# Strassen's scheme for the first FFN product of the last two groups of 512 tokens, in an fp32 attention and FFN kernel

## The chip, the cores and the metric

The kernel runs on one core of a Trainium2 chip. Its engines work side by side (in the profiled run of the kernel before TensorE is busy 96% of the span, VectorE 61% and GpSimd 46%) and are written short in the profiles: TensorE is PE (matmuls) and PEld (its loading of weights), VectorE is DVE, ScalarE is ACT, GpSimd is POOL. SBUF is the memory that holds their operands, and PSUM the one that holds the sums of the matmuls. The metric is device time in microseconds (us) of one execution. A time quoted here is the median of a kernel's runs.

## The reference

```python
batch, n_heads, seq, head_dim = 8, 8, 576, 64         # q, k, v in fp32
n_tokens, d_model, d_ff = 4608, 512, 2048

scores = q @ k.T / 8
scores = where(scores >= max(scores) - tau, scores, -1e9)
attn = exp(scores - max(scores)); attn /= sum(attn) + 1e-9
x = (attn @ v), heads joined: 4608 x 512
h = x @ w_in                                          # 4608 x 2048, the first product
g = where(h > 0, h, exp(min(h, 0)) - 1)               # ELU
out = g @ w_out                                       # the second product
```

## The kernel before

TensorE works in fp32. The kernel cuts the 4608 tokens into nine **groups** of 512, and each group into two **blocks** of 256. Attention of one batch element and the FFN of earlier groups are interleaved by hand. When attention ends, two groups are left, which are computed with nothing else to do: this is the **tail** of the kernel, and the change acts in it alone.

The PSUM pools: the score tile is one tile of four slices of 512 columns, `f` has three separate tiles of 512 columns, `t` has one.

```python
    banks.close()
    for name, bufs in (("s", 1), ("f", 3), ("t", 1)):
        psum[name] = ctx.enter_context(tc.tile_pool(name=f"ps_{name}2", bufs=bufs, space=PSUM))
```

The first product of a block, plainly: for a **unit** `u` (slices `u` and `u + 8` of the 16 slices of the hidden layer) 8 matmuls of 128x128 by 256 columns, then the ELU in three steps on three engines.

```python
    def ffn1(c, u):                       # c: block, u: unit
        def part(k):
            ft = u + k * NU
            ...
            for j in range(KJ):
                nc.tensor.matmul(loc["ph"][:, k], w_in_sb[:, j, ft * P : (ft + 1) * P],
                                 xts[g][:, j, hf * CT : (hf + 1) * CT], start=(j == 0), stop=(j == KJ - 1))
        def exp():
            ...
            nc.scalar.activation(loc["g"], loc["h"], AF.Exp)
        def minus():
            nc.gpsimd.tensor_scalar(loc["g"], loc["g"], 1.0, -1.0, ALU.mult, ALU.add)
        def elu():
            nc.vector.scalar_tensor_tensor(loc["g"], loc["g"], 0.0, loc["h"], ALU.min, ALU.max)
            if u % 2 and c >= PLAIN:
                sums(c, u - 1)            # sums of g for the second product, on GpSimd
```

The second product uses Strassen's scheme (in Winograd's form) already: seven products in place of eight, collected in three accumulators X, Y, Z. The same order serves the change.

```python
    ORDER = ((("g", 0, 0), ("w", 0, 0), "X", True), (("g", 1, 1), ("t", 2), "Z", True), (("g", 1, 0), ("w", 1, 0), "X", False),
             (("s", 1), ("t", 0), "Y", True), (("s", 0), ("w", 0, 1), "Z", True), (("s", 2), ("t", 1), "Y", False),
             (("s", 3), ("w", 1, 1), "Z", False))
```

The end of the program:

```python
        finish_units(after, slice(0, None))
        xts[B] = xpool.tile([P, KJ, MAIN], FP32, name="xt")
        nc.sync.dma_start(xts[B], xtail.rearrange("j p n -> p j n"))
        push_ffn(B)
        while pending or units:
            finish_units(ffn_halves(1), slice(0, None))
            run_extra(99)
```

## Time and profile before

| | before |
|---|---|
| time, first three of the six runs | 1452.35 us (1450.76 to 1452.42) |
| mean granted clock of TensorE, profiled run | 0.995 |
| tail: first matmul of the last two groups to the last one | 207.2 us |
| first product of one group (512 tokens) | 55.3 us |
| second product of one group | 48.35 us |

"Granted clock" is the share of TensorE's full clock that the hardware grants; it is recorded over the whole run. In the kernel before the record falls to 0.50 in three stretches, of 3.41, 6.83 and 3.41 us, between 149.0 and 193.4 us, and is 1.00 from there to the end of the work. A row of a timeline is: start in us, length in us, engine, source line, operation, output tile and input tiles, shapes, how many records are joined in the row, and in brackets the idle time ahead of it with what ended it. A row of the chain of waits is: start, length, engine, output tile, line. The prediction below shows the lines of this profile that the argument rests on.

### The profile page before, as it was taken

Reading aid. Unit: us, or ns where it says so; the run is one execution under the profiler, and the core shown is the slowest. Engines: PE = TensorE matmul, PEld = TensorE weight load, DVE = VectorE, ACT = ScalarE, POOL = GpSimd, SP = SyncE. Lnnn points to the kernel's source line nnn. Section 1 sums busy time; section 2 is a strip of 40 time slices with the busy share of each in tenths; the row PEclk is TensorE's granted clock in tenths of the full one; section 3 lists DMA queues with packets and bytes.
Section 4 is the critical chain, followed back from the end, with each engine's and each line's share of the span. In section 5 each row is a group of like instructions: output and inputs, shape, how many; then the busy total and the mean of one; then the engine's idle time right before and its main releaser. Section 6 shows DMA issues by size and latency. Waiting matters only on the chain.

```text
span 1449.4 us, 20329 instructions
## 1 busy us (share of the span) xinstructions
PE 1391.5 (96%) x6822; PEld 1037.2 (72%) x6822; DVE 878.9 (61%) x1910; ACT 439.7 (30%) x780; POOL 667.7 (46%) x1194
## 2 busy tenths in 40 slices
PE   7988778999999999999999999999999999999998
PEld 4555534647777777777777777777777778888887
DVE  6887665567676766677676767676767674111111
ACT  5665554323222322223222323232323231100100
POOL 4665554546444454535363626363535443313422
PEclk9999899999999999999999999999999999999999
DMA  4344442177677676667676767666767765100000
GB/s 95 78 93 117 111 123 84 51 193 188 184 185 195 174 202 183 190 181 185 183 197 171 189 190 191 182 189 180 195 182 192 192 172 148 45 15 8 8 15 15
DMA packets 298903, 205.44 MB, mean 142 GB/s; under 512 B 206384, under 2 KB 270384, under 8 KB 298800
## 3 DMA queue, kind: packets, MB, share of 16 engines
q1 hardware_dynamic: 298800, 204.15, 52.9%
q8 instruction: 54, 0.88, 0.2%
q14 instruction: 49, 0.40, 0.1%
HBM read 119.87 MB, written 84.21 MB: 141 GB/s over the span
## 4 chain that ended last, share of the span: by engine, by line
PE 82%; DVE 8%; POOL 4%; ACT 3%; issue 2%; DMA 1%; SPq 0%; POOLq 0%; DVEq 0%; ACTq 0%
PE ph L393 33%; PE po L494 24%; PE sc L220 12%; PE pv L347 8%; DVE w L247 2%; PE pv L343 2%; PE po L459 2%; ACT e L235 2%; POOL wtop L141 2%; DVE mx L230 2%; PE rt L259 1%; POOL w L256 1%; DVE wtop L136 1%; POOL nb L231 1%; DVE w_out_sb L145 1%
## 5 line engine op out<-in xcount | busy, mean ns | idle before, releaser
L393 PE MATMUL ph<-xt,w_in_sb 128*128 128x256 f32 x2304 | 521.5, 383 | 3.5 <-DVE w_in_sb L145 3.5
L393 PEld LDWEIGHTS ph<-xt,w_in_sb 128*128 128x128 f32 x2304 | 433.3, 190 | 83.9 <-issue 21.0
L235 ACT ACTIVATE e<-sc,nb,keep 128x576 f32<-128x576 f32 x288 | 227.6, 829 | 439.2 <-POOL nb L231 438.0
L230 DVE TENSOR_REDUCE mx<-sc 128x2 f32<-128x1152 f32 (+1 forms) x176 | 199.9, 1136 | 229.1 <-PE sc L220 229.0
L256 POOL TENSOR_SCALAR w<-w,rs 128x576 f32<-128x576 f32 x288 | 219.1, 771 | 223.5 <-DVE rs L250 217.3
L247 DVE SCALAR_TENSOR_TENSOR w<-sc,th,e 128x576 f32<-128x576 f32 x288 | 226.8, 815 | 78.3 <-ACT e L235 53.8
L220 PE MATMUL sc<-kT,qT 64*128 64x288 f32 x1024 | 180.3, 437 | 18.9 <-DVE w L247 9.1
L404 POOL TENSOR_SCALAR g<-g 128x512 f32<-128x512 f32 x144 | 89.7, 623 | 200.5 <-ACT g L401 199.3
L307 DVE STREAM_TRANSPOSE x<-w 128x512 f32<-128x512 f32 (+1 forms) x350 | 181.2, 567 | 0.9 <-POOL w L256 0.9
L231 POOL TENSOR_SCALAR nb<-mx,nkeep 128x2 f32<-128x2 f32 (+1 forms) x176 | 51.7, 294 | 265.1 <-DVE mx L230 257.6
L401 ACT ACTIVATE g<-ph 128x512 f32<-128x512 f32 x144 | 86.0, 597 | 266.2 <-PE ph L393 266.2
L408 DVE SCALAR_TENSOR_TENSOR g<-g,ph 128x512 f32<-128x512 f32 x144 | 97.0, 674 | 112.7 <-POOL g L404 112.6
L220 PEld LDWEIGHTS sc<-kT,qT 64*128 64x128 f32 x1024 | 99.3, 189 | 86.0 <-issue 53.1
L494 PE MATMUL po<-t,s 128*128 128x256 f32 x512 | 122.8, 386 | 4.5 <-DVE u L514 4.5
L494 PE MATMUL po<-w_out_sb,s 128*128 128x256 f32 x512 | 120.1, 384 | 0.0
L494 PE MATMUL po<-w_out_sb,g 128*128 128x256 f32 x512 | 117.7, 379 | 0.0
L494 PEld LDWEIGHTS po<-t,s 128*128 128x128 f32 x512 | 94.5, 190 | 28.9 <-DVE u L514 8.9
L494 PEld LDWEIGHTS po<-w_out_sb,s 128*128 128x128 f32 x512 | 95.4, 190 | 19.7 <-issue 4.7
L494 PEld LDWEIGHTS po<-w_out_sb,g 128*128 128x128 f32 x512 | 97.3, 190 | 13.9
L424 POOL TENSOR_TENSOR s<-g 128x256 f32<-128x256 f32 x128 | 93.2, 728 | 12.9 <-DVE g L408 12.9
L347 PE MATMUL pv<-wTb,vm 128*64 128x320 f32 x512 | 76.7, 439 | 0.0
L350 ACT COPY xt<-pv 128x256 f32<-128x256 f32 x64 | 23.8, 372 | 159.3 <-PE pv L347 159.2
(64 smaller groups left out, 1129.0 us busy)
## 6 DMA issues: line engine op xcount, KB each, us to landing
there<-x SPq DMA_DIRECT2D x500, 144.0 KB, 3.5
wTb<-there SPq DMA_DIRECT2D x75, 576.0 KB, 4.4
wTa<-there SPq DMA_DIRECT2D x50, 576.0 KB, 3.7
qm<-in_q_dram SPq DMA_DIRECT2D x128, 72.0 KB, 2.6
km<-in_k_dram SPq DMA_DIRECT2D x128, 72.0 KB, 3.6
vm<-in_v_dram SPq DMA_DIRECT2D x64, 128.0 KB, 2.5
wst<-in_moe_w_in_dram SPq DMA_DIRECT2D x16, 512.0 KB, 4.2
wst<-in_moe_w_out_dram SPq DMA_DIRECT2D x16, 512.0 KB, 3.8
```

The source lines that it names most:

```text
L220: nc.tensor.matmul(scs[h][:, a, :HALF], qs[r], kT[r, k0 : k0 + HALF], start=True, stop=True)
L230: nc.vector.tensor_reduce(st["mx"][:, cs], src[:, :, :, :HALF], axis=AX.XY, op=ALU.max)
L235: nc.scalar.activation(e, st[h][:, :, :HALF], AF.Exp, bias=st["nb"][:, h : h + 1], scale=keep)
L247: nc.vector.scalar_tensor_tensor(wv, sc[:, :, :HALF], st["th"][:, h : h + 1], e, ALU.is_ge, ALU.mult, accum_out=sm[:, h : h + 1])
L256: nc.gpsimd.tensor_scalar(wv, wv, st["rs"][:, h : h + 1], 1.0, ALU.mult, ALU.mult)
L307: nc.vector.transpose(x[:, :, c0 : c0 + nc_], src.rearrange("p (c g n) -> p g c n", c=nc_, n=T))
L347: nc.tensor.matmul(pv[h * D : (h + 1) * D, g0 * T : g1 * T], vm[:, h, c], wT[:, g0:g1, h * (NC + 1) + c], start=False, stop=(c == NC - 1), ...
L393: nc.tensor.matmul(loc["ph"][:, k], w_in_sb[:, j, ft * P : (ft + 1) * P], xts[g][:, j, hf * CT : (hf + 1) * CT], start=(j == 0), stop=(j = ...
L404: nc.gpsimd.tensor_scalar(loc["g"], loc["g"], 1.0, -1.0, ALU.mult, ALU.add)
L408: nc.vector.scalar_tensor_tensor(loc["g"], loc["g"], 0.0, loc["h"], ALU.min, ALU.max)
L424: nc.gpsimd.tensor_tensor(out, x, y, op)
L494: nc.tensor.matmul(cur[c, place], lhs, rhs, start=(begins and u == 0), stop=(u == NU - 1), skip_group_check=True)
```

## The change

The first product of the last two groups goes by the seven products as well, for 512 tokens at a time. That needs, per unit, three new sums of weights and one in place (`first_sums`), four sums of the input per group (`input_sums`), and per unit six sums and two copies of the results in PSUM ahead of the ELU. The tiles that attention leaves free (`qm`, `km`, `qT`, `kT`, `e`, `w`, `vm`, `wTa`, `wTb`) hold the sums. Bookkeeping and the second product's small changes are cut.

```diff
@@ at the end of the program
+        def first_sums(u):
+            f0, f1 = (slice(f * P, (f + 1) * P) for f in (u, NU + u))
+            a11, a12, a21 = w_in_sb[:, :2, f0], w_in_sb[:, 2:, f0], w_in_sb[:, :2, f1]
+            s1, s2, s4 = sums_in[u] = [rooms.pop(0).rearrange("p (k f) -> p k f", k=2) for _ in range(3)]
+            nc.vector.tensor_tensor(s1, a21, w_in_sb[:, 2:, f1], ALU.add)
+            nc.vector.tensor_tensor(s2, s1, a11, ALU.subtract)
+            nc.vector.tensor_tensor(a21, a11, a21, ALU.subtract)
+            nc.vector.tensor_tensor(s4, a12, s2, ALU.subtract)
+
+        for u in range(5):
+            first_sums(u)
         while pending or units:
             finish_units(ffn_halves(1), slice(0, None))
             run_extra(99)
 ...
+        def input_sums(g):
+            (b11, b12), (b21, b22) = ...
+            nc.vector.tensor_tensor(t3, b22, b12, ALU.subtract)
+            nc.vector.tensor_tensor(t2, t3, b11, ALU.add)
+            nc.vector.tensor_tensor(t4, b21, t2, ALU.subtract)
+            nc.vector.tensor_tensor(b12, b12, b11, ALU.subtract)
+
+        def first_product(g, u):
 ...
+            if u % 2:
+                sc = psum["s"].tile([P, 2, 2, 512], FP32, name="sc").rearrange("p a b n -> p (a b) n")
+                X, Y, Z = (sc[:, i, :CT] for i in range(3))
+            else:
+                X, Y, Z = (psum["f"].tile([P, 512], FP32, name="po", tag="f")[:, :CT] for i in range(3))
 ...
+            product(a11, b11, X, True)
+            p1 = kept("s1", X)                        # copy on ScalarE
+            product(a22, t4, Z, True)
+            w1 = kept("w1", Z, p1)                    # sum on VectorE, as u2 and t5
+            product(a12, b21, X, False)
+            nc.scalar.copy(h[:, 0, 0], X)
+            product(s2, t2, Y, True)
+            u2 = kept("u2", Y, p1)
+            product(s1, t1, Z, True)
+            t5 = kept("t5", Z, p1)
+            product(s3, t3, Y, False)
+            nc.vector.tensor_tensor(h[:, 0, 1], Y, w1, ALU.add)
+            nc.vector.tensor_tensor(h[:, 1, 1], Y, t5, ALU.add)
+            product(s4, b22, Z, False)
+            nc.vector.tensor_tensor(h[:, 1, 0], Z, u2, ALU.add)
+            for c in range(2):
+                ...
+                nc.scalar.activation(gt, hc, AF.Exp)
+                nc.gpsimd.tensor_scalar(gt, gt, 1.0, -1.0, ALU.mult, ALU.add)
+                nc.vector.scalar_tensor_tensor(gt, gt, 0.0, hc, ALU.min, ALU.max)
+            if u % 2:
+                sums(2 * g, u - 1)
+                run_extra(99)
+
+        input_sums(B - 1)
 ...
+        for g in (B - 1, B):
+            ...
+            for u in range(NU):
+                if g < B and u + 2 in range(5, NU):
+                    first_sums(u + 2)
+                first_product(g, u)
+            ... second products of both blocks; input_sums(B) after the first group's first block
```

More of the change, by code (lines that the diff above doesn't have):

```diff
@@ L397, in exp @@
             if u == 0:
-                gs[c] = gpool.tile([P, NU, 2, 2, P], FP32, name="g")
-            loc["g"] = gs[c][:, u].rearrange("p j i t -> p (j i t)")
+                gs[c] = [gpool.tile([P, NU, 2, 2, P], FP32, name="g")]
+            loc["g"] = hidden(c, u, 1).rearrange("p u j i t -> p (u j i t)")
             loc["h"] = loc["ph"].rearrange("p k t -> p (k t)")
@@ L412, in ffn1, with hidden, sums @@
         return [lambda: part(0), lambda: part(1)], (exp, minus, elu)
-    def sums(c, u):
-        g = gs[c]
+    def hidden(c, u, n):
+        for g in gs[c]:
+            if u < g.shape[1]:
+                return g[:, u : u + n]
+            u -= g.shape[1]
+    def sums(c, u, engines=(nc.gpsimd,) * 4):
+        g = hidden(c, u, 2)
         def one(k):
@@ L419, in one @@
                 ss[c] = late["x"].tile([P, 4, NU, P], FP32, name="s", bufs=1)
-            (a11, a21), (a12, a22) = ([g[:, u : u + 2, j, i] for i in range(2)] for j in range(2))
+            (a11, a21), (a12, a22) = ([g[:, :, j, i] for i in range(2)] for j in range(2))
             s1, s2, s3, s4 = (ss[c][:, i, u : u + 2] for i in range(4))
@@ L423, in one @@
                              (s3, a11, a21, ALU.subtract), (s4, a12, s2, ALU.subtract))[k]
-            nc.gpsimd.tensor_tensor(out, x, y, op)
+            engines[k].tensor_tensor(out, x, y, op)
         extra.extend((0.8, c, lambda k=k: one(k)) for k in range(4))
@@ L458, in run @@
             for ft in range(4 * part + 2 * k, 4 * part + 2 * k + 2):
-                nc.tensor.matmul(cur[c, i][:, :DM], gs[c][:, ft % NU, ft // NU, i], w_out_sb[:, ft],
+                nc.tensor.matmul(cur[c, i][:, :DM], hidden(c, ft % NU, 1)[:, 0, ft // NU, i], w_out_sb[:, ft],
                                  start=(ft == 0), stop=(ft == NFT - 1))
@@ L488, in part @@
             for u in range(k * NU // 2, (k + 1) * NU // 2):
-                lhs = gs[c][:, u, left[1], left[2]] if left[0] == "g" else ss[c][:, left[1], u]
+                lhs = hidden(c, u, 1)[:, 0, left[1], left[2]] if left[0] == "g" else ss[c][:, left[1], u]
                 if right[0] == "w":
@@ L548, in behind @@
             values(pr, 0 if i == 1 else 1)
-        if i == NB - 1 and (pr + 1) % NPAIR == 0:
+        if i == NB - 1 and (pr + 1) % NPAIR == 0 and pr + 1 < NP:
             push_ffn(pr // NPAIR)
@@ L693, with pieces_of @@
         finish_units(after, slice(0, None))
-        xts[B] = xpool.tile([P, KJ, MAIN], FP32, name="xt")
-        nc.sync.dma_start(xts[B], xtail.rearrange("j p n -> p j n"))
-        push_ffn(B)
+        def pieces_of(pool, name, shape, n, times=1, bufs=None):
+            for _ in range(times):
+                t = pool.tile(shape, FP32, name=name, bufs=bufs)
+                if len(shape) > 2:
+                    axes = " ".join("abc"[: len(shape) - 1])
+                    t = t.rearrange(f"p {axes} -> p ({axes})")
+                for x in range(0, t.shape[1] - n + 1, n):
+                    yield t[:, x : x + n]
+        QN = 2 * P
+        rooms = [*pieces_of(raw, "qm", [P, S // T, T], QN), *pieces_of(raw, "km", [P, S // T, T], QN),
+                 *pieces_of(qkp, "qT", [P, S], QN, 2), *pieces_of(qkp, "kT", [P, TAIL + S], QN, 2),
+                 *pieces_of(att, "e", [P, 2, HALF], QN, 2), *pieces_of(wpool[0], "w", [P, 2 * S], QN)]
+        sums_in = {}
+        def first_sums(u):
[8 more added lines that the diff above has]
+            first_sums(u)
         while pending or units:
@@ L699 @@
             run_extra(99)
+        wide, narrow = wtp.tile([P, 3 * NT, NCH, T], FP32, name="wTb"), wtp.tile([P, 2 * NT, NCH, T], FP32, name="wTa")
+        wide, narrow = (t.rearrange("p g c n -> p (g c n)") for t in (wide, narrow))
+        g2 = [t.rearrange("p (u j i t) -> p u j i t", j=2, i=2, t=P) for t in (wide[:, : 12 * QN], narrow[:, : 4 * QN])]
+        rooms += [wide[:, 12 * QN : 13 * QN], narrow[:, 8 * QN : 9 * QN], *pieces_of(raw, "vm", [P, 2, NC, D], QN, bufs=2)]
+        t2, t4 = (narrow[:, x * QN : (x + 2) * QN].rearrange("p (k t) -> p k t", k=2) for x in (4, 6))
@@ new lines @@
+        (t3,) = pieces_of(raw, "vm", [P, 2, NC, D], 2 * QN, bufs=2)
+        t3 = t3.rearrange("p (k t) -> p k t", k=2)
+        hs = [h.rearrange("p (c j t) -> p c j t", c=2, j=2) for h in pieces_of(late["x"], "x", [P, NT, NCH, T], 4 * QN, 2, 2)]
+        def input_sums(g):
+            (b11, b12), (b21, b22) = ([xts[g][:, k : k + 2, t : t + CT] for t in (0, CT)] for k in (0, 2))
+            nc.vector.tensor_tensor(t3, b22, b12, ALU.subtract)
+            nc.vector.tensor_tensor(t2, t3, b11, ALU.add)
+            nc.vector.tensor_tensor(t4, b21, t2, ALU.subtract)
+            nc.vector.tensor_tensor(b12, b12, b11, ALU.subtract)
@@ new lines, in first_product, with product, kept @@
+        def first_product(g, u):
+            f0, f1 = (slice(f * P, (f + 1) * P) for f in (u, NU + u))
+            (b11, t1), (b21, b22) = ([xts[g][:, k : k + 2, t : t + CT] for t in (0, CT)] for k in (0, 2))
+            s1, s2, s4 = sums_in[u]
+            a11, a12, s3, a22 = w_in_sb[:, :2, f0], w_in_sb[:, 2:, f0], w_in_sb[:, :2, f1], w_in_sb[:, 2:, f1]
+            if u % 2:
[3 more added lines that the diff above has]
+                X, Y, Z = (psum["f"].tile([P, 512], FP32, name="po", tag="f")[:, :CT] for i in range(3))
+            h = hs[u % 2]
+            def product(left, right, place, begins):
+                for k in range(2):
+                    nc.tensor.matmul(place, left[:, k], right[:, k], start=(begins and k == 0), stop=(k == 1),
+                                     skip_group_check=True)
+            def kept(name, x, y=None):
+                t = epool.tile([P, HM], FP32, name=name)
+                if y is None:
+                    nc.scalar.copy(t, x)
+                else:
+                    nc.vector.tensor_tensor(t, x, y, ALU.add)
+                return t
+            product(a11, b11, X, True)
[14 more added lines that the diff above has]
+            for c in range(2):
+                gt = hidden(2 * g + c, u, 1).rearrange("p u j i t -> p (u j i t)")
+                hc = h[:, c].rearrange("p j t -> p (j t)")
+                nc.scalar.activation(gt, hc, AF.Exp)
[4 more added lines that the diff above has]
+                run_extra(99)
@@ new lines @@
+        input_sums(B - 1)
+        xts[B] = xpool.tile([P, KJ, MAIN], FP32, name="xt")
+        nc.sync.dma_start(xts[B], xtail.rearrange("j p n -> p j n"))
+        for g in (B - 1, B):
+            gs[2 * g] = [gpool.tile([P, NU, 2, 2, P], FP32, name="g")]
+            gs[2 * g + 1] = g2
+            for u in range(NU):
+                if g < B and u + 2 in range(5, NU):
+                    first_sums(u + 2)
+                first_product(g, u)
+            for c in (2 * g, 2 * g + 1):
+                units.extend((ffn2, (c, m)) for m in range(7))
+                if c % 2:
+                    for u in range(0, NU, 2):
+                        sums(c, u, (nc.vector, nc.vector, nc.gpsimd, nc.vector))
+                    run_extra(99)
+                while pending or units:
+                    finish_units(ffn_halves(1), slice(0, None))
+                if c == 2 * B - 2:
+                    input_sums(B)
```

## The prediction

> **What bounds the kernel now.** I read the page's busy shares first, then the clock of the cores, then the chain of waits over the last 300 us, then the timeline of the end of attention. The page says that PE is busy nearly all the time, and the chain says where this change acts:
>
> ```profile
> PE 1391.5 (96%) x6822; PEld 1037.2 (72%) x6822; DVE 878.9 (61%) x1910; ACT 439.7 (30%) x780; POOL 667.7 (46%) x1194
> ...
> 1237.77 27.63 PE ph L393 x128
> 1265.40 24.17 PE po L494 x112
> 1289.57 27.63 PE ph L393 x128
> 1317.19 24.17 PE po L494 x112
> 1341.37 27.63 PE ph L393 x128
> 1368.99 24.17 PE po L494 x112
> 1393.17 27.63 PE ph L393 x128
> 1420.80 24.19 PE po L494 x112
> ```
>
> The first line is of the page, the others of the chain: start, length, engine, line, records. After attention come four blocks, one for each 256 tokens: first product (ph, 128 records), then second product (po, already Strassen's, 112). From 1237.77 to 1444.98 PE waits for nothing. One fp32 matmul of 128x128 by 256 columns is two records, so a record takes 27.63/128 = 0.2159 us and a matmul 0.432 us. In this tail a saved matmul is saved time, and a PE stall is lost time.
>
> The other engines are nearly idle there, so their durations matter only where PE waits for them. The groups of the window 1235 to 1449 (mean ns after the comma):
>
> ```profile
> L408 DVE SCALAR_TENSOR_TENSOR g<-g,ph 128x512 f32<-128x512 f32 x32 | 22.0, 687 | 94.9 <-POOL g L404 94.9
> L404 POOL TENSOR_SCALAR g<-g 128x512 f32<-128x512 f32 x32 | 19.7, 617 | 132.5 <-ACT g L401 132.5
> L401 ACT ACTIVATE g<-ph 128x512 f32<-128x512 f32 x32 | 19.1, 597 | 135.3 <-PE ph L393 135.3
> L514 DVE TENSOR_TENSOR w<-po,s 128x256 f32<-128x256 f32 x4 | 1.7, 425 | 19.8 <-PE po L494 19.8
> L512 ACT COPY s<-po 128x256 f32<-128x256 f32 x4 | 1.5, 372 | 11.6 <-PE po L494 11.6
> ```
>
> What a real wait costs PE is seen where one happens, at 1154 in the timeline:
>
> ```profile
> 1150.50 3.62 PE L494 MATMUL po<-w_out_sb,s 128*128 128x256 f32 x16
> 1154.06 0.40 DVE L514 TENSOR_TENSOR u<-po,s 128x256 f32<-128x256 f32 x1
> 1154.52 1.59 PEld L494 LDWEIGHTS po<-t,s 128*128 128x128 f32 x8 [0.81 <-DVE u L514]
> 1154.52 1.99 PE L494 MATMUL po<-t,s 128*128 128x256 f32 x8 [0.41 <-DVE u L514]
> ...
> 1231.55 0.41 DVE L504 TENSOR_TENSOR ot<-po,w 128x256 f32<-128x256 f32 x1
> ...
> 1237.61 12.68 PE L393 MATMUL ph<-xt,w_in_sb 128*128 128x256 f32 x58
> 1237.81 0.42 DVE L504 TENSOR_TENSOR ot<-po,u 128x256 f32<-128x256 f32 x1 [5.84 <-PE po L494]
> ```
>
> DVE ends at 1154.46, PE starts 0.06 later, and its eight records last 1.99 instead of the 1.89 of unstalled groups of eight: 0.10 more, as the weights were not loaded ahead. A last record ends 0.379 after its start, and a waiting reader starts 0.04 after that. The last three lines show that DVE has nothing to do from 1231.96 until the last product of group 6 ends at 1237.8.
>
> [...] in the tail here the granted clock is 1.00, while 150 to 160 us shows 0.67. [...]
>
> **The change, part by part.** (a) *Removed:* per unit u (two of 16 slices of the hidden layer, 512 tokens) 7 products of two matmuls stand in place of 16 matmuls. 2 groups x 8 units x 2 matmuls x 0.432 = **-13.8 us**. Nothing in attention changes: the two groups were already computed after it.
>
> (b) *Start.* DVE gets 20 weight sums (5 units x 4) ahead of its last output sum. They start at 1231.96. Dependent ones follow after 0.45 us, independent ones after 0.34 (1231.21 to 1231.55): (0.45+0.34+0.45+0.34) x 5 = 7.9, to 1239.9. Then come the output sum to 1240.3 and three dependent input sums of 512 elements, 0.69+0.03 each, to 1242.4. PE does the first product from 1237.77 to 1238.63, and the second needs the third of those sums. PE waits until 1242.5: **+3.9 us**.
>
> (c) *Even units* take their three accumulators X, Y, Z from three separate PSUM tiles. With PE at full rate products start every 0.863 us. The previous unit's ELU (sum h, ACT 0.60, POOL 0.62, DVE 0.69) leaves DVE 2.7 us in; w1 is done by 3.15, needed at 3.45; the copy of X is done by 1.66, needed at 1.73; u2 and t5 have 0.18 us to spare. About 6.04 us, no stall.
>
> (d) *Odd units* take X, Y, Z as three slices of **one** PSUM tile, the former score tile. I built the changed kernel and looked up to which instruction each semaphore value belongs. In an odd unit every product after the first waits for the *reading of the product before it*, though that is in another slice:
>
> ```
> Z  = a22*t4   waits ACT: copy s1 of X
> X += a12*b21  waits DVE: w1 of Z
> Y  = s2*t2    waits ACT: copy of X
> Z  = s1*t1    waits DVE: u2 of Y
> Y += s3*t3    waits DVE: t5 of Z
> Z += s4*b22   waits DVE: both sums of Y
> ```
>
> In even units only the wait for the slice's own reader is there. So an odd unit is serial. A product after a wait: 0.10 + 3x0.216 + 0.379 = 1.13 to its end, 0.04 to the reader, 0.425 (DVE) or 0.372 (ACT), 0.06 back: 1.65 or 1.60 from start to start. The first step is 1.72, as ACT still has the previous exponential; the one with two sums is 1.65+0.34. Sum: 1.72+1.65+1.60+1.65+1.65+1.99 + last product 0.96 = 11.2 us, against 6.04. If ACT is free it is 11.0. So 5.1 x 8 odd units = **+40.8 us**.
>
> (e) In units 3, 4, 5 of the first group four more weight sums (1.6 us) stand before w1. DVE, free at 2.7, starts w1 at 4.3 instead of 2.8: about 1.4 us of stall each, **+4.2 us**.
>
> (f) [...] ELU sums now read two SBUF operands beside GpSimd, and unit 4's weight sums run beside four GpSimd sums of 0.73. A choice, not a reading: **+1.5 us**.
>
> (g) Second product: for odd blocks the sums now start only when the block before has ended, 12 dependent-ish DVE sums (5 us) after up to 3.2 us of other sums. First needed after three products of 16 records, 10.4 us. Hidden: 0.
>
> Sum: -13.8 + 3.9 + 40.8 + 4.2 + 1.5 = +36.6 us, so 1452.35 + 36.6 = **1489 us**, 2.5% slower.
>
> **Rivals.** *The saving survives:* if the waits of odd units were hidden, (a) to (c) and (e) would give 1452 - 13.8 + 8 = 1447, within 2%. For it speaks that DVE and ACT are mostly idle in the tail. Against it speak the waits in the built program: idle engines don't help when PE alternates with them. *A new bound on DVE:* per unit six sums and two ELU operations are 6x0.425+2x0.69 = 3.9 us of 6.04, so DVE isn't the bound; only its order matters, as in (b) and (e). *The clock:* PE idles 3.8 us at the start, and odd units leave it 54% busy (6.04 of 11.2). If windows were throttled, odd units would lose more: a halved clock over one odd unit would add up to 6 us. Between 200 and 230 us, where PE is 64 to 83% busy with waits, the clock is 1.00, so I expect at most one or two such windows. [...]
>
> **Range and chances.** Odd units could be 0.5 us off each, +-4 us; (b) and (e) +-2[...]. So 1481 to 1497. The 2% line is at 1481.4, at the low end of this: slower by over 2% 0.88, within 2% 0.10, faster by over 2% 0.02 (it would need more than the whole saving).
>
> **What would show it.** Right: first-product units after attention alternate between some 6 and 11 us; in odd ones PE waits five or six times 0.7 to 0.8 us for DVE and ACT in turn; before the first group's second product PE waits about 4 us for an input sum; units 3 to 5 are about 1.4 us longer; the second-product blocks stay at 24.2 us; PE's matmul count falls by 64 records. Wrong: if odd units take about 6 us, (d) is wrong and the time is near 1447; if the chain shows GpSimd or the granted clock falls in the tail, (f) or the clock was undersized.

## The result

| | before | after |
|---|---|---|
| median of 6 runs | 1452.38 us (1450.76 to 1454.83) | 1504.03 us (1502.53 to 1507.68) |
| ratio | | 1.036, 95% interval 1.0344 to 1.0376 |
| mean granted clock, profiled run | 0.995 | 0.982 |
| tail | 207.2 us | 259.0 us |
| first product of group 1, group 2 of the tail | 55.3, 55.3 us | 91.7, 70.6 us |
| second product per group | 48.35 us | 48.35 us |

Both give the right result, as all kernels below do. A ratio is the mean time of one kernel's fast runs over the mean time of the other's in the same rounds, so it is not quite the ratio of the medians. The change is slower by 3.6%, and the whole of it lies in the tail: 259.0 - 207.2 = 51.8 us, against 1504.03 - 1452.38 = 51.65 of the medians. The time is above the predicted range.

The page of the kernel after, the busy shares and the clock in 40 slices of the span (tenths, 9 is full):

```profile
PE 1411.8 (94%) x6758; PEld 1031.8 (69%) x6758; DVE 951.1 (63%) x2070; ACT 451.2 (30%) x812; POOL 659.2 (44%) x1170
...
PEclk9999999999999999999999999999999999699999
```

PE has 64 records fewer and is busy 20 us longer. This sounds contradictory. Of the 20 us, 14 lie in the tail (221.4 us busy against 207.4), and the rest ahead of it, where two executions differ. In the tail there are two reasons. The second line shows one: in one slice near the end, 37.6 us wide, the clock was 0.6 on average, and at half clock (recorded as 0.50) records start 0.427 us apart in place of 0.216. The other is that a product of four records that stands between waits counts as 1.03 to 1.13 us busy (below), while in an unbroken row a product takes 0.86.

The chain of waits over the tail. Of the rows at line 762, `po` names even units, whose accumulators are three tiles, and `sc` names odd ones, whose accumulators are slices of one tile:

```profile
1333.72 48.35 PE po L500 x224
1382.06 6.06 PE po L762 x28
...
1399.54 6.32 PE po L762 x28
```

In group 2 an even unit is one unbroken piece of 28 records and 6.06 to 6.32 us. The next even unit starts 17.5 us later, so the odd unit between takes 11.4, and the chain breaks it into single products. The second product of a group, the row of 224 records at line 500, is as long as before. The timeline of PE, the first product of the tail that waits (first line) and one odd unit of group 2:

```profile
1245.99 2.01 PE L762 MATMUL po<-wTa,w_in_sb 128*128 128x256 f32 x4 [3.09 <-DVE wTa L745]
...
1387.94 1.03 PE L762 MATMUL sc<-xt,w_in_sb 128*128 128x256 f32 x4
1389.60 1.13 PE L762 MATMUL sc<-wTa,w_in_sb 128*128 128x256 f32 x4 [0.64 <-ACT s L768]
1391.47 1.13 PE L762 MATMUL sc<-xt,w_in_sb 128*128 128x256 f32 x4 [0.74 <-DVE w L770]
1393.06 1.13 PE L762 MATMUL sc<-wTa,qT 128*128 128x256 f32 x4 [0.46 <-ACT x L778]
1394.78 1.13 PE L762 MATMUL sc<-xt,km 128*128 128x256 f32 x4 [0.59 <-DVE u L770]
1396.43 1.13 PE L762 MATMUL sc<-vm,w_in_sb 128*128 128x256 f32 x4 [0.52 <-DVE t L770]
1398.41 1.13 PE L762 MATMUL sc<-xt,qT 128*128 128x256 f32 x4 [0.85 <-DVE x L785]
```

Each product waits for the reader of the product before it, ScalarE and VectorE in turn. The six waits sum to 3.80 us, and each waiting product lasts 1.13 in place of 1.03. The first line also shows the other thing: four records of 2.01 us, where others take 1.03 to 1.13. The clock record is 0.50 there, from 1246.09 to 1249.50.

Where the clock was half is read from the table by windows. Its columns are: window, its length, busy time of PE, PEld, DVE, ACT and POOL (with records), granted clock, share of DMA, GB/s. The clock record changes only at multiples of 3.413 us (in this trace its half-clock stretches last 3.41, 6.83, 13.65 and 17.07 us), so I cut the windows there. This is unit 3 of group 1:

```profile
1273.39:1276.81 3.42, 1.18 (x5) 0.68 (x4) 2.19 (x6) 0.00 (x0) 0.00 (x0) 1.00 0.00 0
1276.81:1280.22 3.41, 2.37 (x5) 1.47 (x6) 0.42 (x1) 0.37 (x1) 0.00 (x0) 0.50 0.02 5
1280.22:1283.63 3.41, 2.89 (x7) 1.82 (x7) 0.42 (x1) 0.00 (x0) 0.00 (x0) 0.50 0.00 0
...
1287.05:1290.46 3.41, 3.41 (x10) 2.69 (x9) 2.11 (x3) 1.00 (x2) 1.67 (x3) 0.50 0.00 0
1290.46:1293.87 3.41, 2.02 (x10) 1.44 (x8) 3.38 (x7) 0.37 (x1) 2.43 (x3) 1.00 0.00 0
```

Here a window in which PE did little (first line: 1.18 us) is followed by half clock, and the half clock lasts until after a window that PE filled (the one from 1287.05: 3.41). PE did little there because VectorE was doing six sums, four of them weight sums for a later unit; the wait in the timeline is this:

```profile
1275.67 1.13 PE L762 MATMUL sc<-xt,w_in_sb 128*128 128x256 f32 x4 [2.23 <-DVE w L770]
```

The lengths of the first-product units, from the start of their first record to that of the next unit's:

| unit | 0 | 1 | 2 | 3 | 4 | 5 | 6 | 7 |
|---|---|---|---|---|---|---|---|---|
| group 1, us | 11.09 | 11.44 | 6.31 | 16.60 | 9.29 | 17.55 | 7.84 | 11.57 |
| group 2, us | 6.04 | 11.43 | 6.31 | 11.41 | 6.31 | 11.41 | 6.31 | 11.41 |

In the tail there are three such stretches: 3.41 us after the start wait, 13.65 us from unit 3 on and 17.07 us from unit 5 on; 34.1 us in all, every one in group 1. Group 2 has the same odd units without weight sums, and its clock is 1.00 throughout.

To compare windows I use one more quantity below, the **share** of a window in which PE's array works. I work it out from the records: each is counted as 0.427 us at half clock, which is how far apart they start there in the kernel after, and as half of that, 0.213, at full clock, where 0.216 is measured; the sum is divided by 3.413. The busy column is larger, as a record is shown 0.379 us long where the next one starts 0.216 us after it. The share is an estimate, good to a few hundredths.

### The profile page after: what moved, and what is told of

It is laid out like the page before. It is cut to its first block, busy times and chain, and to the rows that moved or that the text cites. A ratio compares the mean times of both kernels' runs of the same rounds, so it can differ in the third digit from the quotient of the medians.

```text
span 1505.5 us, 20487 instructions
## 1 busy us (share of the span) xinstructions
PE 1411.8 (94%) x6758; PEld 1031.8 (69%) x6758; DVE 951.1 (63%) x2070; ACT 451.2 (30%) x812; POOL 659.2 (44%) x1170
## 4 chain that ended last, share of the span: by engine, by line
PE 80%; DVE 9%; POOL 4%; ACT 3%; issue 2%; DMA 1%; SPq 0%; DVEq 0%; POOLq 0%; ACTq 0%
PE ph L393 25%; PE po L500 22%; PE sc L220 12%; PE pv L347 8%; PE sc L762 4%; PE po L762 3%; PE po L465 2%; PE pv L343 2%; DVE w L247 2%; ACT e L235 2%; DVE mx L230 2%; PE rt L259 2%; POOL wtop L141 2%; POOL w L256 1%; DVE wtop L136 1%
## 5 line engine op out<-in xcount | busy, mean ns | idle before, releaser
L393 PE MATMUL ph<-xt,w_in_sb 128*128 128x256 f32 x1792 | 409.3, 383 | 3.2 <-DVE w_in_sb L145 3.2
L393 PEld LDWEIGHTS ph<-xt,w_in_sb 128*128 128x128 f32 x1792 | 335.3, 190 | 70.2 <-issue 21.0
L220 PE MATMUL sc<-kT,qT 64*128 64x288 f32 x1024 | 183.4, 442 | 19.2 <-DVE w L247 9.6
L401 ACT ACTIVATE g<-ph 128x512 f32<-128x512 f32 x112 | 66.9, 597 | 131.0 <-PE ph L393 131.0
L500 PE MATMUL po<-w_out_sb,g 128*128 128x256 f32 x448 | 103.2, 379 | 0.0
L404 POOL TENSOR_SCALAR g<-g 128x512 f32<-128x512 f32 x112 | 70.0, 625 | 68.1 <-ACT g L401 67.0
L500 PEld LDWEIGHTS po<-w_out_sb,g 128*128 128x128 f32 x448 | 85.1, 190 | 12.2
L408 DVE SCALAR_TENSOR_TENSOR g<-g,ph 128x512 f32<-128x512 f32 x112 | 75.0, 670 | 17.8 <-POOL g L404 17.7
L430 POOL TENSOR_TENSOR s<-g 128x256 f32<-128x256 f32 x112 | 81.7, 730 | 0.0
L792 POOL TENSOR_SCALAR g<-g 128x512 f32<-128x512 f32 x16 | 9.9, 618 | 152.6 <-ACT g L791 152.6
```

Of the source, the lines that this page charges most:

```text
L220: nc.tensor.matmul(scs[h][:, a, :HALF], qs[r], kT[r, k0 : k0 + HALF], start=True, stop=True)
L430: engines[k].tensor_tensor(out, x, y, op)
L500: nc.tensor.matmul(cur[c, place], lhs, rhs, start=(begins and u == 0), stop=(u == NU - 1), skip_group_check=True)
```

## The experiments

**Theory.** Two separate costs add up: the odd units are serial because three accumulators are slices of one PSUM tile, which costs 5.4 us per unit; and where VectorE's weight sums (or the start's sums) lengthen one wait, the array's share of one window falls below some limit, and the clock halves for one to five windows. **Rivals.** The odd units are slow for some other reason, VectorE or ScalarE themselves, so that separate tiles don't help. Or the clock falls because serial units run PE at half duty for long, whatever the single wait is. Or the clock falls only from a gap of a certain length.

Kernels of one call were compared with the kernel before on the same chip: 1453.68 us beside the first four, 1452.76 beside the last four. The tail is the cleaner number: the start of the tail varied by 4 us either way between profiled executions, with the early part of attention, where the clock record is 0.50 for 13.7 us in the kernel before and for 20.5 in the kernel after.

| kernel | median us | ratio to before, 95% | tail us | first product of group 1, 2 | clock |
|---|---|---|---|---|---|
| e1_split | 1454.29 | 1.001, 0.9989 to 1.003 | 210.2 | 62.5, 51.0 | 0.991 |
| e2_pool_loop | 1497.44 | 1.0307, 1.0282 to 1.0332 | 250.3 | 82.9, 70.7 | 0.988 |
| e3_pool_all | 1498.45 | 1.0313, 1.0282 to 1.0344 | 247.2 | 79.8, 70.7 | 0.987 |
| e4_split_pool | 1445.66 | 0.9951, 0.9927 to 0.9975 | 202.3 | 54.6, 51.0 | 0.995 |
| e5_gaps_g2 | 1520.53 | 1.0466, 1.0448 to 1.0483 | 273.9 | 91.9, 85.3 | 0.974 |
| e6_minus_dve | 1442.50 | 0.9922, 0.9906 to 0.9938 | 197.8 | 52.0, 49.1 | 0.995 |
| e7_early | 1445.34 | 0.9944, 0.9929 to 0.996 | 200.5 | 52.7, 51.1 | 0.989 |
| e8_both | 1441.74 | 0.9915, 0.9896 to 0.9934 | 196.0 | 50.2, 49.1 | 0.987 |

### e1_split: three PSUM tiles for the odd units too

The score pool is closed when attention has ended, and three separate tiles take its place. Nothing else differs from the kernel after.

```diff
-    for name, bufs in (("s", 1), ("f", 3), ("t", 1)):
-        psum[name] = ctx.enter_context(...)
+    score_banks = ExitStack()
+    for name, bufs in (("f", 3), ("t", 1), ("s", 1)):
+        psum[name] = (score_banks if name == "s" else ctx).enter_context(...)
 ...
-                sc = psum["s"].tile([P, 2, 2, 512], FP32, name="sc").rearrange("p a b n -> p (a b) n")
-                X, Y, Z = (sc[:, i, :CT] for i in range(3))
+                X, Y, Z = (psum["o"].tile([P, 512], FP32, name="sc")[:, :CT] for _ in range(3))
 ...
+        score_banks.close()
+        psum["o"] = ctx.enter_context(tc.tile_pool(name="ps_o", bufs=3, space=PSUM))
         input_sums(B - 1)
```

> Only the odd units' three accumulators change: three one-bank PSUM tiles in place of three slices of one tile; every sum stays where it is. Theory (the shared tile makes odd units serial, 5.2 us each): odd units fall from 11.4 to about 6.3 us, 8 x 5.2 = 41 us are gained; the start still costs 3.1 us and its slow-clock window about 1.8; the weight sums in units 3 to 5 leave gaps of 1.4 us between busy stretches, [...] so the 12 us of slow clock in units 3 to 6 go too: about 1452 us (1447 to 1457), clock 1.00 from unit 1 on. Rival (the seven products depend on DVE and ACT anyway; the tile is not the cause): odd units stay above 10 us, time above 1490.

Measured: 1454.29 us, the tail 210.2 in place of 259.0. An odd unit of group 2 takes 6.21 to 6.23 us in place of 11.41. The timeline of PE, the last four products of one:

```profile
1356.42 1.06 PE L762 MATMUL sc<-xt,w_in_sb 128*128 128x256 f32 x4
1357.32 1.03 PE L762 MATMUL sc<-wTa,qT 128*128 128x256 f32 x4
1358.23 1.13 PE L762 MATMUL sc<-xt,km 128*128 128x256 f32 x4
1359.19 1.03 PE L762 MATMUL sc<-vm,w_in_sb 128*128 128x256 f32 x4
```

The brackets with idle time are gone: products start 0.9 us apart, on the same operands and with the same readers. So the one tile was the cause of the odd units' length, and neither VectorE nor ScalarE was. Even units became a little longer, 6.71 in place of 6.31, as the other engines now have 6.2 us in place of 11.4 for an odd unit's work.

The start held a surprise that matters below. The expectation gave its wait a slow window, as in the kernel after. The wait was there, as long as before, and no slow window followed:

```profile
1241.92 1.13 PE L762 MATMUL po<-wTa,w_in_sb 128*128 128x256 f32 x4 [3.10 <-DVE wTa L746]
```

In the kernel after and in two kernels below the same wait, 3.08 to 3.09 us, lies almost wholly in one window, leaves it a share of 0.05 to 0.13, and half clock follows. Here the end of a window (at 1240.04) fell into the wait; the two windows that share it keep 0.59 and 0.41, and the clock stayed at 1.00.

Another thing was missed: unit 4 of group 1 took 12.24 us, far from a normal unit. The timeline there, all engines:

```profile
1272.01 0.90 POOL L430 TENSOR_TENSOR s<-g 128x256 f32<-128x256 f32 x1
...
1272.37 0.83 DVE L724 TENSOR_TENSOR w<-w,w_in_sb 128x256 f32<-128x256 f32 x1
...
1274.78 2.08 PE L762 MATMUL po<-xt,e 128*128 128x256 f32 x4 [3.34 <-DVE w L770]
```

VectorE's weight sums last 0.83 us in place of 0.42, beside GpSimd's sums for the second product. PE waits 3.34 us for VectorE, which comes to `w1` only after them. The share of the window from 1270.8 on is 0.15, and the clock was half for the next two, 6.8 us.

### e2_pool_loop: the weight sums of units 5 to 7 on GpSimd

From the kernel after, with one tile as there. The three calls in the loop move from VectorE to GpSimd, into odd units.

```diff
-        def first_sums(u):
+        def first_sums(u, engine=nc.vector):          # four nc.vector.tensor_tensor become engine.tensor_tensor
 ...
-                if g < B and u + 2 in range(5, NU):
-                    first_sums(u + 2)
+                if g < B and u in (1, 3, 5):
+                    first_sums(u // 2 + 5, nc.gpsimd)
```

> Odd units stay serial; only the 12 weight sums that stood before w1 in units 3 to 5 of the first group go to GpSimd, issued after units 0, 2 and 4, so the 2.2 us PE gaps of units 3 and 5 shrink to 0.8. Theory (PE's clock was halved because of those long gaps): clock 1.00 from unit 1 on, the first group's block takes as long as the second's (70.6) plus the start's 3.1 and 1.8: 75.5 in place of 91.7, time about 1488 (1484 to 1492). Rival (the low duty of serial units by itself halves the clock, wherever its window falls): stretches at 0.5 remain in odd units, time above 1495.

Measured: 1497.44 us, 6.6 better than the kernel after. This misses the 1488 that followed from my theory in its first form, and the rival's number was met. But the rival's mechanism isn't what happened: the odd units of group 2 are as serial, and their clock was 1.00 throughout. The sums on GpSimd lengthened VectorE's ELU from 0.69 to 1.20 us, so that `w1` was still late, and one slow stretch was left in unit 3. The wait there, and two windows from the same place:

```profile
1272.37 1.13 PE L762 MATMUL sc<-xt,w_in_sb 128*128 128x256 f32 x4 [1.30 <-DVE w L770]
```

```profile
1270.89:1274.30 3.41, 1.65 (x7) 0.99 (x7) 1.43 (x2) 0.37 (x1) 2.96 (x4) 1.00 0.00 0
1274.30:1277.71 3.41, 2.82 (x7) 1.79 (x6) 0.42 (x1) 0.00 (x0) 0.00 (x0) 0.50 0.02 5
```

Unit 5 has nearly the same wait, 1.29 us, and unit 1 has it too, and neither was slowed. They differ in how they lie in the windows: the share of the window with the wait is 0.33 in unit 3, 0.42 in unit 5 and 0.39 in unit 1. So the length of one gap alone doesn't decide, and the theory needs the share of a window, not the wait.

### e3_pool_all: the weight sums ahead of the tail on GpSimd as well

```diff
         for u in range(5):
-            first_sums(u)
+            first_sums(u, nc.gpsimd)
```

> As e2_pool_loop, and the 20 weight sums of the start go to GpSimd too, which is idle from 1217 to 1242. Theory: at the start only the output sum and three input sums (2.5 us) stand between PE's last old product and the first t4, of which 0.86 is hidden: the stall falls from 3.1 to about 1.7 and the slow-clock window at the start goes: 1488 - 1.4 - 1.8 = about 1485 (1481 to 1489), clock 1.00 in the whole tail. Rival (the start's halving has nothing to do with the length of the gap): the clock still falls there and the gain is 1.4 at most.

Measured: 1498.45 us, the same as e2_pool_loop within the intervals, and not the expected 1481 to 1489. In the trace the first unit is 8.01 us in place of 11.09 and the slow window at the start is gone (the share there is 0.42 in place of 0.12), so the tail is 3.1 us shorter; the medians don't show it, and the variation of attention can hide that much. The slow stretch in unit 3 remained, behind a window of share 0.32, and the window of share 0.38 in unit 1 had none after it.

### e4_split_pool: separate tiles and all weight sums on GpSimd

This is e1_split with the edits of e2_pool_loop and e3_pool_all.

> e1_split and e3_pool_all together: three PSUM tiles in odd units, all weight sums on GpSimd. Theory: 1452.4 - 13.8 + 1.7 (start) + 16 units x 0.3 (late w1 [...]) = about 1445 (1441 to 1449), faster than the kernel before by 0.5%, clock 1.00. Rival (the first product by Strassen cannot pay, because each unit waits on sums anyway): 1452 or more.

Measured: 1445.66 us, 0.5% faster than before. The clock is 1.00 through the whole tail, odd units take 6.21 to 6.74 us, and unit 4 of group 1 is 6.73 in place of e1's 12.24. First products take 54.6 and 51.0 us against 55.3. So with both costs taken away the saving appears; together they return 56.7 us of tail (259.0 - 202.3).

### e5_gaps_g2: dummy sums on VectorE in group 2

From the kernel after: group 2, whose clock was full there, gets four sums that nobody reads in units 3 and 5. If waits that empty a window are the cause, slow stretches must appear where there were none; if the serial units are, nothing more than the direct wait can.

```diff
+        dummy = epool.tile([P, HM], FP32, name="dm")
 ...
+                if g == B and u in (3, 5):
+                    for _ in range(4):
+                        nc.vector.tensor_tensor(dummy, w_out_sb[:, 0, : 2 * P], w_out_sb[:, 1, : 2 * P], ALU.add)
                 first_product(g, u)
```

> The changed kernel with one thing added: four idle sums (128x256, two SBUF operands, result unused) on DVE before w1 in units 3 and 5 of the second group, where the clock was 1.00 throughout; the first group has four real weight sums there and its clock halved. Theory (the clock halves where PE is active for less than about 0.35 of one of its 3.41 us windows, and an odd unit then stays slow because at half clock it never fills a window): the second group shows slow stretches of 7 to 17 us beginning in units 3 and 5, and its first-product block grows from 70.6 by 2 x 1.8 of waiting and about 2 x 5 of slow clock to 80 to 86 us; time 1513 to 1519. Rival (the first group's slow clock comes from the start or from something else in that group): the second group stays at 1.00 and grows by about 3.6 us, time about 1508.

Measured: 1520.53 us, 1.5 us above the expected range; group 2's first product takes 85.3 us in place of 70.6, within its range. The windows at unit 3 and at unit 5 of group 2:

```profile
1403.41:1406.82 3.41, 1.13 (x4) 0.68 (x4) 2.66 (x6) 0.52 (x2) 1.06 (x2) 1.00 0.00 0
1406.82:1410.23 3.41, 2.23 (x5) 1.32 (x5) 0.67 (x2) 0.37 (x1) 0.00 (x0) 0.50 0.00 0
...
1430.71:1434.12 3.41, 0.97 (x5) 0.68 (x4) 2.38 (x6) 0.00 (x0) 0.00 (x0) 1.00 0.00 0
1434.12:1437.54 3.42, 2.48 (x6) 1.17 (x4) 0.38 (x1) 0.37 (x1) 0.00 (x0) 0.50 0.00 0
```

The four sums need 8 x 0.42 = 3.4 us in both units together, and PE's wait for `w1` grows by as much (2.43 and 2.44 us in place of 0.74); the first product grew by 14.7. The remaining 11.3 us are half clock, in two stretches that the kernel after doesn't have. This is the direct proof of the clock's part: the wait creates the slow stretch, and the stretch costs about three times the wait.

### e6_minus_dve: the ELU's subtraction on VectorE

From e4_split_pool, to measure what it costs there that instructions of VectorE and GpSimd last longer beside each other (in the kernel after the ELU lasts 1.20 us beside GpSimd's sums and 0.69 alone).

```diff
-                nc.gpsimd.tensor_scalar(gt, gt, 1.0, -1.0, ALU.mult, ALU.add)
+                nc.vector.tensor_scalar(gt, gt, 1.0, -1.0, ALU.mult, ALU.add)
```

> e4_split_pool with the ELU's subtraction of 1 on DVE instead of GpSimd, both halves. Theory (in e4 a unit takes 6.7 us in the first group and 6.4 in the second, not 6.04, [...]: subtraction 1.03 instead of 0.62, ELU 1.20 instead of 0.69, so w1 is late): [...] units fall towards 6.1 to 6.4: 3 to 5 us faster than e4, about 1441.5. Rival (DVE gets too full[...]): same as e4 or slower, 1445 to 1450.

Measured: 1442.50 us, 0.8% faster than before. The groups of instructions in the tail's first products (count, busy us, mean ns, idle before), in e4_split_pool:

```profile
L793 DVE SCALAR_TENSOR_TENSOR wTb<-wTb,x 128x512 f32<-128x512 f32 x12 | 12.9, 1077 | 6.2 <-POOL wTb L792 6.2
L792 POOL TENSOR_SCALAR wTb<-wTb 128x512 f32<-128x512 f32 x12 | 12.2, 1017 | 2.3 <-ACT wTb L791 2.3
```

and in e6_minus_dve:

```profile
L793 DVE SCALAR_TENSOR_TENSOR wTb<-wTb,x 128x512 f32<-128x512 f32 x12 | 10.7, 894 | 0.4
L792 DVE TENSOR_SCALAR wTb<-wTb 128x512 f32<-128x512 f32 x12 | 5.0, 418 | 0.0
```

These lines are the second half of the ELU in units 0 to 5 (output `wTb`). Its subtraction takes 418 ns on VectorE in place of 1017 on GpSimd, and VectorE no longer waits for it (6.2 us before, 0.4 now). In the first half (output `g`) the subtraction takes 466 ns in place of 621. Although VectorE has more work, units become shorter: 6.72 to 6.23 us for even ones of group 2, 6.21 to 6.08 for odd ones. The tail gains 4.5 us. This edit takes away three things at once: GpSimd's longer subtraction, the handing over to GpSimd and back, and a part of the lengthening of the two engines' instructions beside each other. How much of the 4.5 us is due to the last isn't separated.

### e7_early: the input sums ahead of the last output sum

From e4_split_pool: there PE still waits 1.71 us at the start of the tail for the input sums, which stand behind the drain of the previous group on VectorE.

```diff
-        while pending or units:
-            finish_units(ffn_halves(1), slice(0, None))
-            run_extra(99)
 ...
         input_sums(B - 1)
+        while pending or units:
+            finish_units(ffn_halves(1), slice(0, None))
+            run_extra(99)
```

> e4_split_pool with the input sums of the first group put ahead of the last output sum of group 6 on DVE, so that they run while PE finishes it. Theory: the start's stall of 1.7 us falls to 0 to 0.2: about 1444.0, and PE shows no gap before the second product. Rival (the sums then delay that output sum and with it a PSUM tile): the stall moves to the third product (Y) and less than 0.8 us is gained.

Measured: the wait is gone (first unit 6.17 us in place of 8.01) and the tail is 1.8 us shorter. The ratio, 0.9944 against 0.9951, doesn't show it: a gain of 1.8 us, 0.12%, is within the intervals.

### e8_both: e6_minus_dve and e7_early together

> e6_minus_dve and e7_early together, as the candidate for the best version. Theory: gains add: about 1440 (1437 to 1443), clock 1.00 in the whole tail, 0.8% faster than the kernel before; the floor by counting matmuls alone is 1452.4 - 13.8 = 1438.6. Rival: one of the two parts does not hold, 1444 or more.

Measured: 1441.74 us, 0.85% faster than before and 4.1% faster than the kernel after. Its tail is the shortest, 196.0 us; by time it can't be told from e6_minus_dve. The chain of its tail:

```profile
1241.07 6.17 PE po L759 x28
1247.24 6.04 PE sc L759 x28
```

An even and an odd unit are now one piece each, 6.17 and 6.04 us. The first products of both groups take 50.2 + 49.1 = 99.3 us against 2 x 55.3 before: 11.2 us of the 13.8 that the arithmetic saves. The rest is in short waits behind GpSimd's weight sums in units 3 and 5 (6.6 us each) and in some 0.2 us in even units.

## Why the prediction was right or wrong

The direction and the larger part of the size were right. The time was 15 us above the predicted 1489, and the range ended at 1497, 8 us above it, an allowance for the clock and for (f) by estimate. The sum, term by term, in the tail (the groups' unit lengths give the measured column):

| term | predicted us | measured us |
|---|---|---|
| (a) fewer matmuls | -13.8 | -13.8: an unstalled unit takes 6.04, PE has 64 records fewer |
| (b) start | +3.9 | +3.2: a wait of 3.09 and 0.10 to resume |
| (c) even units | 0 | +1.6: 6.31 in place of 6.04 in six of them |
| (d) odd units | +40.8 | +43.0: 11.41 each |
| (e) weight sums in units 3 to 5 | +4.2 | +4.7 |
| (f) VectorE beside GpSimd | +1.5 | inside (c), (d) and (e) |
| clock | 0 | +13.2 |
| sum | +36.6 | +51.9, against 51.8 of the two tails |

The measured sum meets the tails by its making, as the clock's 13.2 is what the other terms leave; the check of it stands below. Without the clock the terms sum to +38.7, or 1491 us, 2 from the prediction.

**The serial odd units (d): right, shown.** e1_split changed the tiles alone and took 11.41 us to 6.21. The 0.2 us above the predicted 11.2 lie in one step: the third product starts 1.87 us after the second, where 1.65 was worked out, because `w1` stands on VectorE behind an ELU that waits for a GpSimd subtraction of 0.98 us in place of 0.62. The other steps came within 0.07 of the working.

**The start (b) and the weight sums (e): right in kind and nearly in size.** The waits are as described; three times about 1.5 us in units 3 to 5, and 0.2 in unit 7. The start's 20 sums took 7.3 us (1236.14 to 1243.47) and not 7.9: of each four only the second follows after 0.45 us, the others after 0.34, where the working gave two the longer step.

**VectorE beside GpSimd (f): too small.** The choice of 1.5 us was an estimate, for ELU sums and unit 4's weight sums. A sign of it ahead of the result was line 145 of the kernel before, 128x512 on VectorE: 685 to 694 ns in all eleven that ran while GpSimd was idle, 743 to 1231 in nine of the twenty-one beside it. In the kernel after, GpSimd's subtraction in the second half of the ELU went from 0.62 to about 1.0 us where VectorE worked on the ELU's first half, VectorE's ELU in its turn from 0.69 to 1.20 beside GpSimd's sums, and the weight sums from 0.42 to between 0.83 and 0.94 beside them. With serial units most of this was hidden. With separate tiles it counts: e6_minus_dve, which takes the subtraction off GpSimd, gains 4.5 us, though not all of that need be the lengthening.

**The clock: the step that failed.** The rivals' part put it as "so I expect at most one or two such windows", and the sum had nothing for it. Ten windows were slow. Group 1's first product is 91.7 - 70.6 = 21.1 us longer than group 2's; less the waits of (b) and (e), 3.2 + 4.7, this leaves 13.2 us. A second way agrees: in the nine slow windows of units 3 to 6 the shares sum to 6.48, so the array worked 22.1 us there, of which full clock would have saved half, 11.1; the first unit has 11.09 - 6.04 - 3.2 = 1.85 more. Two things were wrong in the step. It took comfort from attention, where PE is busy 64 to 83% and the clock 1.00 (200 to 230 us of the kernel before), and carried that to the *average* of an odd unit (54%). The average was in fact harmless: group 2's odd units ran at clock 1.00 with windows down to a share of 0.44. What went with half clock was the single poorest window (0.25 and 0.30 ahead of the two long stretches), and term (e) had already placed a wait into the middle of a serial unit, without asking what share was left there. And the prediction treated a slow window as one window. Once slow, it lasted here: the serial products at half clock filled 0.51 to 0.74 of a window, after which the clock stayed at half, and it came back only after a window that an even unit filled (share 1.00).

In the tails of all kernels run here, 12 windows were followed by half clock (not counting the program's end), and their shares lie between 0.05 and 0.33. The lowest that were not are 0.38, 0.39, 0.40 and 0.41. Windows at half clock were followed by full clock at 0.83 and above, and not at 0.77 and below. That the wait causes the slow stretch is shown, by adding it (e5_gaps_g2) and by taking it away (e4_split_pool). That the length of the wait alone doesn't decide is shown by the start: 3.08 to 3.09 us in three kernels with half clock after it, 3.10 in e1_split with none; and in e2_pool_loop half clock followed a window whose longest wait was 1.30 us. So where a window ended within a wait was part of the cost here. One would expect that executions of one kernel then differ in their slow windows; as one execution of each was profiled, that isn't shown. Where exactly the limits lie is only bracketed. It also holds only for these matmuls: in the early part of attention, with transposes and small matmuls among the records, my share doesn't separate windows (drops follow shares from about 0.1 to 0.7 there), and I left that open.

**The second product (g): right.** 48.35 us per group in every kernel.

**The rival "the saving survives":** its 1447 was worked out for hidden waits in odd units. e4_split_pool, which hides them, gave 1445.66.

## What to carry to other kernels

When a producer and several readers take turns on slices of one PSUM tile, look in the built program at which reader each matmul waits for; separate tiles for separate accumulators were worth 5.2 us per odd unit here, where moving the readers' work to another engine was worth at most 0.5 per unit (e6_minus_dve against e4_split_pool). When waits are put into work on TensorE that is already serial, count how much of each 3.4 us window is left to the array (here half clock followed shares of 0.33 and less, and none followed 0.38 and more), and give the slow clock that follows a line of its own in the sum: here 3.4 us of added waits cost 14.7. Then read the engine next to it: a helper engine that is mostly idle can still be the wrong place, if it lengthens the instructions of the one that the matmuls wait for: here VectorE's weight sums went from 0.42 to between 0.83 and 0.94 us, its ELU from 0.69 to 1.20. And a wait costs more than its own length: in the odd unit of group 2 shown above PE started 0.05 to 0.06 us after the end of the reader and took 0.10 more for the product (1.13 in place of 1.03), and 1.6 to 2.0 us passed from one product to the next in place of 0.86.
